# RWKV-7 and top-k experts: quarters of each triangular inverse joined on TensorE, and one fixed order of instructions per engine

## The chip, the cores and the metric

The kernel runs on one core of one Trainium2 chip. The metric is the device time of one execution in microseconds (us), the lower the better. A core has TensorE (PE; its weight loads are listed as PEld), VectorE (DVE), ScalarE (ACT), GpSimd (POOL) and SyncE (SP), which issues most of the DMAs.

## What is computed

Two blocks follow each other. The first is a recurrence over 768 time steps for 4 batches and 8 heads of 40 dimensions:

```python
for t in range(S):
    y[:, :, t] = np.einsum('bhd,bhde->bhe', rt, state)
    Sa = np.einsum('bhde,bhe->bhd', state, at)
    state_decay = state * wt[:, :, None, :] - np.einsum('bhd,bhe->bhde', Sa, bt)
    state = state_decay + np.einsum('bhd,bhe->bhde', vt, kt)
```

Its output, 3072 rows of 320, is the input of the second: each row goes to the expert (of 8) with the largest logit of `x @ w_gate`; each expert keeps the 80 rows with the largest softmax weight; their output is that weight times `relu(x @ w1[e]) @ w2[e]`, and every other row is zero. All is in fp32.

## The kernel before

**Chunks.** The time axis is cut into 12 chunks of T = 64 steps, and two batches (z = 0, 1) lie side by side on the 128 partitions. A unit is one chunk of one pair of batches: 24 units, of which every second one continues the same state. Within a chunk the recurrence becomes linear algebra with a unit triangular system per batch and head. This system is solved by blocks of C = 32: the two 32 x 32 diagonal blocks are inverted, and substitution takes three products (`diagonal(0)`, `below`, `diagonal(1)`).

**Stages of a unit.** `prepare`: transposes of w and a, running products of the decay (`pt`, a scan on VectorE), their reciprocal `ip` (L251), the scaled b and k (`ub`, `kh`, on POOL), their transposes, and the scores against `ahT`, evicted by ACT into `nt` and masked by POOL (L221). `solve`: transposes of r and v, the transposed state (`gT`), the right side (L362, L366), copied to `yy`, the three products (L385, L376, L385), each followed by a copy into `u` (VectorE) or `yy` (ACT), and the new state (L396, L402, L403). `outputs`: the transpose of u, a second set of scores (`lam`, masked on POOL), their products (L441, L448), the multiplication into `xT` (L452), and one matmul (L459) that turns the result back into rows and gives the partial logits. `gate` takes four units at a time: softmax, arg-max, and the largest weights per expert by ten rounds of max and match-replace. It also writes the rows, with the weight as a column, to DRAM.

**Inversion.** Four units together have 128 diagonal blocks (2 batches x 2 blocks x 4 units x 8 heads), one to a partition. `system` writes the blocks from `nt` to DRAM, `invert` reads them back as `lt`, and step i does one product and one sum on VectorE:

```python
nc.vector.tensor_tensor(out=tm, in0=t3[:, 0:i, i : i + 1]..., in1=l3[:, i : i + 1, i + 1 :]..., op=Alu.mult)
nc.vector.tensor_tensor(out=t3[:, 0:i, i + 1 :], in0=t3[:, 0:i, i + 1 :], in1=tm, op=Alu.add)
```

With i = 1 to 30 that is 60 instructions of 30 to 240 elements per partition, six times. The inverse goes to DRAM (`solved`) and comes back as `dt`, laid out for TensorE.

**Order.** The loop over n issues, by `woven`, pieces of `solve(n)`, `outputs(n - 1)`, `prepare(n + 6)`, half an inversion in two of four passes, and a gate. Each list of pieces is spread evenly over the pass. The scheduler of the programming layer sets the final order on each engine, so that blocks of one kind of matmul are often cut by others. In the last passes, `keep_at_work` adds dummy matmuls (L133). Transposes, `gT`, `pp`, the logits and the dummies share two PSUM buffers (`ps_t`).

**End.** After the loop the best weights per expert are merged, slots are computed, rows are gathered by index and the experts' products are done (L715 to L732), with 18 MB of weights loaded in the meantime.

Of the kernel before, what the change touches and what calls it, by code (L numbers as in the profile page):

```python
# [18 lines left out]
def kernel(  # L19
# [26 lines left out]
    nc = tc.nc  # L46
# [24 lines left out]
    XG = 2 * DM - NF * 128  # L71
    XW = XG + 1
# [50 lines left out]
    gates = const.tile([128, NM, E], F32, name="gates")  # L123
    ids = const.tile([128, NM, E], F32, name="ids")
# [11 lines left out]
    with ExitStack() as p1:  # L136
        AHEAD = NG + 2
        NK = AHEAD + 2
        hold = p1.enter_context(tc.tile_pool(name="hold", bufs=1))
        kept = p1.enter_context(tc.tile_pool(name="kept", bufs=NK))  # L140
# [6 lines left out]
        early = dict(w=w, a=a, k=k, b=b)  # L147
        late = dict(r=r, v=v)
# [13 lines left out]
        raw = {n: padded(f"raw_{n}", 2, [128, H, HB], 1.0 if n == "w" else 0.0, dims) for n in (*early, *late)}  # L162
# [4 lines left out]
        state = padded("state", BP, [128, Z, G, 2, HB])  # L167
        og_t = padded("og", 2, [128, NG, 32])
        cand = padded("cand", 2, [128, capr + ZT])

        units = [(c, bp) for c in range(NC) for bp in range(BP)]
        halves = [slice(T * z, T * (z + 1)) for z in range(Z)]

        def load(n, src):
            c, bp = units[n]
            for name, ap in src.items():
                for z in range(Z):
                    nc.sync.dma_start(raw[name][n % 2][halves[z], :, 0:D],
                                      ap[Z * bp + z, :, c * T : (c + 1) * T, :].rearrange("h t d -> t h d"))
# [21 lines left out]

        def scores(lhs, rhs):

            p = ps_s.tile([128, 2, 2, G, T], F32, name="sp", tag="s")
            for i in range(2):
                for g in range(G):
                    for z in halves:
                        for q in range(2):
                            m = slice(HB * q, HB * (q + 1))
                            nc.tensor.matmul(p[z, q, i, g, :], lhsT=lhs[i][m, g, z], rhs=rhs[m, g, z],  # L210
                                             start=True, stop=True)
            return p
# [10 lines left out]

        blocks = nc.dram_tensor("blocks", (NCI, Z, NS, NG, H, C * C), F32, kind="Internal")
        solved = nc.dram_tensor("solved", (NCI, Z, NS, NG, H, C * C), F32, kind="Internal")
        xb_lg = {}
        made = {}
        inverse = {}
        rows_x = {}

        def prepare(n):

            s = {}

            def decays():
                s["raw"] = [raw[x][n % 2] for x in early]
                dec = decay[n % 2]
                nc.scalar.copy(dec[:, :, :, 1:], by_batch(transposed(pairs(s["raw"][0]))))  # L238

                s["pt"] = pt = kept.tile([128, G, Z, T + 1], F32, name="pt", tag="pt")  # L240
                nc.vector.tensor_tensor_scan(flat(pt), flat(dec), flat(begins), 0.0, op0=Alu.mult, op1=Alu.add)  # L241

            def inverted():
                pt = s["pt"]
                p = ps_t.tile([128, G, 2 * D], F32, name="pp", tag="t")
                for g in range(G):
                    for z in range(Z):
                        nc.tensor.matmul(p[halves[z], g, :], lhsT=pt[:, g, z, 1:], rhs=pick[:, 0, 0 : 2 * D],  # L248
                                         start=g == 0, stop=True, skip_group_check=True)
                s["ip"] = ip = sb.tile([128, H, D], F32, name="ip", tag="ip")  # L250
                nc.vector.reciprocal(ip, p.rearrange("p g (q d) -> p (g q) d", q=2))  # L251
                ub, kh = ubs[n % NK], khs[n % NK]
                nc.gpsimd.tensor_tensor(out=ub[:, :, 0:D], in0=s["raw"][3][:, :, 0:D], in1=ip, op=Alu.mult)  # L253
                nc.gpsimd.tensor_tensor(out=kh[:, :, 0:D], in0=s["raw"][2][:, :, 0:D], in1=ip, op=Alu.mult)
                if n + 2 < len(units):
                    load(n + 2, early)

            def decayed_a():
                s["ahT"] = ahT = kept.tile([128, G, ZT], F32, name="ahT", tag="ahT")
                nc.vector.scalar_tensor_tensor(out=by_batch(ahT), in0=by_batch(transposed(pairs(s["raw"][1]))),  # L260
                                               scalar=-1.0, in1=s["pt"][:, :, :, 0:T], op0=Alu.mult, op1=Alu.mult)

            def operand_b():
                s["ubT"] = copied("ubT", pairs(ubs[n % NK]), 1)

            def operand_k():
                s["khT"] = copied("khT", pairs(khs[n % NK]), 1)

            def system():
                nt = kept.tile([128, 2, 2, G, T], F32, name="nt", tag="nt")  # L270
                evicted(nt, scores((s["ubT"], s["khT"]), s["ahT"]))
                masked(nt, slice(1, 2))
                made[n] = s["pt"], s["ahT"], ubs[n % NK], khs[n % NK], nt

                for z in range(Z):
                    for i in range(NS):
                        tt = slice(i * C, (i + 1) * C)
                        p = slice(z * T + i * C, z * T + (i + 1) * C)
                        nc.sync.dma_start(blocks[n // NG, z, i, n % NG].rearrange("h (s t) -> s h t", s=C),
                                          nt[p, 0].rearrange("p q g t -> p (q g) t")[:, :, tt])  # L280
            return [(2, decays), (3, decayed_a), (2, inverted), (2, operand_b), (2, operand_k), (4, system)]

        def invert(k):

            s = {}

            def begin():
                s["lt"] = lt = sb.tile([128, C * C], F32, name="lt", tag="lt", bufs=1)
                nc.sync.dma_start(lt, blocks[k].rearrange("z i u h x -> (z i u h) x"))
                l3 = lt.rearrange("p (s t) -> p s t", s=C)  # L290
                nc.gpsimd.affine_select(out=l3, in_=l3, compare_op=Alu.is_gt, fill=0.0, base=0,
                                        pattern=[[-1, C], [1, C]], channel_multiplier=0)
                s["tt"] = tt = sb.tile([128, C * C], F32, name="tt", tag="tt", bufs=1)
                nc.scalar.copy(tt, lt)  # L294
                nc.gpsimd.memset(tt[:, 0 :: C + 1], 1.0)

            def step(i):
                l3 = s["lt"].rearrange("p (s t) -> p s t", s=C)
                t3 = s["tt"].rearrange("p (s t) -> p s t", s=C)
                n = C - 1 - i  # L300
                tmp = sb.tile([128, C * C // 4], F32, name="tmp", tag="tmp", bufs=1)
                tm = tmp[:, 0 : i * n].rearrange("p (j t) -> p j t", j=i)
                nc.vector.tensor_tensor(  # L303
                    out=tm, in0=t3[:, 0:i, i : i + 1].to_broadcast([128, i, n]),
                    in1=l3[:, i : i + 1, i + 1 :].to_broadcast([128, i, n]), op=Alu.mult)
                nc.vector.tensor_tensor(out=t3[:, 0:i, i + 1 :], in0=t3[:, 0:i, i + 1 :], in1=tm, op=Alu.add)  # L306

            def end():
                nc.sync.dma_start(solved[k].rearrange("z i u h x -> (z i u h) x"), s["tt"])
                inverse[k] = dt_ = sb.tile([128, NG, 2, G, C], F32, name="dt", tag="dt")  # L310
                for z in range(Z):
                    for i in range(NS):
                        p = z * T + i * C
                        nc.sync.dma_start(dt_[p : p + C].rearrange("p u q g t -> p (u q g) t"),
                                          solved[k, z, i].rearrange("u h (s t) -> s (u h) t", s=C))

            return [(3, begin)] + [(1, lambda i=i: step(i)) for i in range(1, C - 1)] + [(1, end)]

        def staggered(first, second, lead):
            first, second = list(first), list(second)
            order = first[:lead]
            for x in range(max(len(first) - lead, len(second))):
                order += first[lead + x : lead + x + 1] + second[x : x + 1]
            return order

        def solve(n):

            c, bp = units[n]
            s = {}
            st = state[bp]

            def reads():
                s["m"] = made[n]
                s["rT"] = copied("rT", pairs(raw["r"][n % 2]))

            def reads_v():
                s["vT"] = copied("vT", pairs(raw["v"][n % 2]))  # L340

# [65 lines left out]
            def loads():  # L407
                if n + 2 < len(units):
                    load(n + 2, late)
# [366 lines left out]
```

## Time and profile before

| | us |
|---|---|
| three runs, lowest / median / highest | 768.96 / 769.78 / 782.09 |
| the profiled execution | 773.57 |
| its span, first to last instruction | 771.9 |
| TensorE busy in it | 601.9 |
| VectorE busy in it | 411.8 |
| mean granted TensorE clock | 0.837 of full |

A row of the timeline has the start, the length, the engine, the line, the operation, what is written and read, the tile of the array (rows x columns), the shape, and how many records are merged; an entry in brackets is idle time before it and what ended it. An fp32 matmul of the smaller tiles appears as two records. The number at the end of a slice is in tenths. Busy time of TensorE overlaps and is no measure of work; the starts of successive blocks are.

### The profile page before, as it was taken

What the parts mean: (1) busy time and instruction counts of PE and PEld (TensorE: products, weight loads), DVE (VectorE), ACT (ScalarE), POOL (GpSimd) and SP (SyncE); (2) the same over time, 40 slices, a digit from 0 to 9 for tenths busy, and PEclk for the clock granted to TensorE, in tenths of its full rate; (3) what the DMA queues carried; (4) which work ended last, traced back from release to release, by engine and by line L of the source; (5) the groups of instructions that cost most, each with busy time, mean ns of one, the idle gap of its engine ahead of it and who ended that gap; (6) DMA issues with size and microseconds to landing.
All of it is one profiled execution on the core that took longest, in us unless ns stands there. A gap on an engine that the chain in (4) does not pass through costs nothing. (4 is left out here: it accounts for less than half of the span.)

```text
span 771.9 us, 28902 instructions
## 1 busy us (share of the span) xinstructions
PE 601.9 (78%) x13042; PEld 504.9 (65%) x13042; DVE 411.8 (53%) x961; ACT 189.5 (25%) x318; POOL 170.2 (22%) x236
## 2 busy tenths in 40 slices
PE   3645528889899767987989796899989941769997
PEld 2534427777788666876878675777868830667775
DVE  5413943598486954787466884558444148200001
ACT  1322122333344222341323332232222210000000
POOL 3331312322223221231233222221111110010111
PEclk9866667899999887996889988788889975657999
DMA  5545553533455145531455333221320018996000
GB/s 86 118 87 101 124 114 51 117 80 76 90 102 89 33 88 100 93 66 26 83 97 97 57 53 76 47 54 20 74 61 12 4 42 260 351 319 197 24 18 16
DMA packets 224911, 69.50 MB, mean 90 GB/s; under 512 B 205332, under 2 KB 219796, under 8 KB 224788
## 3 DMA queue, kind: packets, MB, share of 16 engines
q1 hardware_dynamic: 216640, 57.18, 35.0%
q10 hardware_dynamic: 7380, 8.68, 3.8%
q8 instruction: 102, 1.67, 0.9%
q0 software_dynamic: 768, 1.81, 0.8%
q14 instruction: 21, 0.17, 0.1%
HBM read 51.85 MB, written 15.77 MB: 88 GB/s over the span
## 5 line engine op out<-in xcount | busy, mean ns | idle before, releaser
L221 POOL TENSOR_SCALAR_AFFINE_SELECT lam<-lam 64x1024 f32<-64x1024 f32 x48 | 55.5, 1155 | 238.7 <-ACT lam L215 237.1
L303 DVE TENSOR_TENSOR tmp<-tt,lt 128x30 f32<-128x30 f32 (+9 forms) x180 | 72.7, 404 | 14.0 <-ACT tt L294 9.3
L306 DVE TENSOR_TENSOR tt<-tt,tmp 128x30 f32<-128x30 f32 (+9 forms) x180 | 74.5, 414 | 5.6 <-DVE tmp L303 0.5
L385 PE MATMUL pr<-yy,dt 32*32 32x40 f32 x1536 | 45.8, 211 | 21.6 <-DMA dt<-solved 10.2
L251 DVE RECIPROCAL ip<-pp 128x320 f32<-128x320 f32 x24 | 51.6, 2150 | 16.4 <-PE pp L248 16.4
L221 POOL TENSOR_SCALAR_AFFINE_SELECT nt<-nt 64x512 f32<-64x512 f32 x48 | 32.9, 685 | 111.4 <-ACT nt L215 106.0
L385 PEld LDWEIGHTS pr<-yy,dt 32*32 32x32 f32 x1536 | 37.3, 117 | 30.4 <-ACT yy L378 12.0
L194 PE MATMUL tp<-ident,ub 128*128 128x128 f32 x96 | 20.7, 353 | 44.4 <-POOL ub L253 44.4
L387 DVE COPY u<-pr 128x320 f32<-128x320 f32 x48 | 23.4, 488 | 55.7 <-PE pr L385 53.4
L734 DVE TENSOR_SCALAR y<-yp,rows 80x320 f32<-80x320 f32 x8 | 4.4, 547 | 77.7 <-PE yp L732 77.7
L452 DVE TENSOR_TENSOR xT<-yp,pt 128x512 f32<-128x512 f32 x24 | 16.5, 687 | 53.5 <-PE yp L448 53.5
L194 PEld LDWEIGHTS tp<-ident,ub 128*128 128x128 f32 x96 | 13.2, 174 | 47.8 <-POOL ub L253 47.7
L241 DVE TENSOR_TENSOR_SCAN pt<-decay,begins 128x520 f32<-128x520 f32 x24 | 30.3, 1261 | 23.5 <-ACT decay L238 23.3
L448 PE MATMUL yp<-lam,kh 64*64 64x64 f32 x768 | 35.8, 248 | 7.7 <-POOL lam L221 7.5
L732 PE MATMUL yp<-w,hT 128*80 128x320 f32 x128 | 38.8, 452 | 0.0
L448 PEld LDWEIGHTS yp<-lam,kh 64*64 64x64 f32 x768 | 27.5, 150 | 15.0 <-POOL lam L221 10.3
L715 PEld LDWEIGHTS hp<-xe,w 128*128 128x128 f32 x256 | 36.1, 227 | 1.4 <-DVE xe L707 1.3
L726 ACT ACTIVATE hT<-hp 128x320 f32<-128x320 f32 x16 | 6.1, 435 | 125.7 <-DMA w<-in_moe_w_dram 63.8
L715 PE MATMUL hp<-xe,w 128*128 128x80 f32 x256 | 36.3, 311 | 0.0
L199 ACT COPY ubT<-tp 128x512 f32<-128x512 f32 x24 | 14.0, 585 | 87.0 <-PE tp L194 87.0
L215 ACT COPY nt<-sp 128x1024 f32<-128x1024 f32 x24 | 24.3, 1012 | 39.2 <-PE sp L210 31.2
L210 PE MATMUL sp<-rT,vT 64*64 64x64 f32 x768 | 31.5, 233 | 3.0 <-ACT nt L215 3.0
(344 smaller groups left out, 1288.6 us busy)
## 6 DMA issues: line engine op xcount, KB each, us to landing
w<-in_moe_w_dram SPq DMA_DIRECT2D x8, 1280.0 KB, 14.7
w<-in_moe_w_dram SPq DMA_DIRECT2D x8, 1024.0 KB, 16.2
x_rows<-xb ACTq DMA_DIRECT2D x48, 96.2 KB, 2.5
raw_w<-in_w_dram SPq DMA_DIRECT2D x48, 80.0 KB, 2.9
raw_a<-in_a_dram SPq DMA_DIRECT2D x48, 80.0 KB, 3.4
raw_k<-in_k_dram SPq DMA_DIRECT2D x48, 80.0 KB, 2.8
raw_b<-in_b_dram SPq DMA_DIRECT2D x48, 80.0 KB, 2.8
out_dram<-zero ACTq DMA_DIRECT2D x8, 480.0 KB, 4.1
```

The source lines that it names most:

```text
L194: nc.tensor.transpose(p[:, g, :], t[:, g, :], ident)
L210: nc.tensor.matmul(p[z, q, i, g, :], lhsT=lhs[i][m, g, z], rhs=rhs[m, g, z], start=True, stop=True)
L215: nc.scalar.copy(o.rearrange("p i q g t -> p q i (g t)"), p.rearrange("p q i g t -> p q i (g t)"))
L221: nc.gpsimd.affine_select(out=oo, in_=oo, compare_op=Alu.is_gt, fill=0.0, base=0, pattern=[[0, oo.shape[1]], [1, T]], channel_multiplier=-1)
L241: nc.vector.tensor_tensor_scan(flat(pt), flat(dec), flat(begins), 0.0, op0=Alu.mult, op1=Alu.add)
L251: nc.vector.reciprocal(ip, p.rearrange("p g (q d) -> p (g q) d", q=2))
L303: nc.vector.tensor_tensor(out=tm, in0=t3[:, 0:i, i : i + 1].to_broadcast([128, i, n]), in1=l3[:, i : i + 1, i + 1 :].to_broadcast([128, i, ...
L306: nc.vector.tensor_tensor(out=t3[:, 0:i, i + 1 :], in0=t3[:, 0:i, i + 1 :], in1=tm, op=Alu.add)
L385: nc.tensor.matmul(pr[m, h, :], lhsT=dt_[m, n % NG, h % 2, h // 2, :], rhs=s["yy"][m, h, :], start=h == 0, stop=True, skip_group_check=True)
L448: nc.tensor.matmul(s["y"][HB * q : HB * (q + 1), z, g, :], lhsT=x[halves[z], 2 * g + q, :], rhs=s["lam"][halves[z], o, q, g, :], start=Fal ...
L715: nc.tensor.matmul(hp[f // (FK // 2)][:, f % (FK // 2), :], lhsT=t1[:, i, f * 128 : (f + 1) * 128], rhs=xe[:, i, :], start=f % (FK // 2) = ...
L732: nc.tensor.matmul(yp, lhsT=hT[:, f, :], rhs=w2[:, f, :], start=f == 0, stop=f == FK - 1)
```

## The change

- **Quarters.** Each 32 x 32 block's two 16 x 16 diagonal quarters are inverted, side by side in one instruction: `step` runs for i = 1 to 14. If A and D are the inverted quarters and B the corner between them, the missing corner is the product A B D. Two sets of 32 small matmuls for each unit form it: `joint_n` (with `an`, the transpose of A, which goes through DRAM as `solved_n`) and `joint`, whose result is added into `dt`.
- **Order.** `do(f, ...)` gives each instruction of TensorE, VectorE, ACT and POOL a dependence on the one before it on its engine. The loop is a list of `do` calls, in which parts of one tiling shape stand together. SP's order is still the scheduler's.
- **State.** The state has 64 columns per pair of heads and not 128; the new state is one addition on VectorE and one product on POOL. A second copy, `state_b`, in the form that the right side needs, is made by two ACT copies (`spread`).
- **Rest.** Units are prepared five passes ahead and not six. Rows are written to DRAM in each pass, by SP, without the weight; the weight comes with the token number out of one matmul of twice the columns. The first loads are issued by SP and ACT in turn. The dummy matmuls in the loop are gone; those after it stay.

The core of the diff:

```diff
+        Q = C // 2
+        state = padded("state", BP, [128, Z, G, HB], 0.0, lambda t: t)
+        state_b = padded("state_b", BP, [128, Z, G, 2, D])
-            return [(3, begin)] + [(1, lambda i=i: step(i)) for i in range(1, C - 1)] + [(1, end)]
+        def step(k, i):
+            l4, t4 = quarters(inverse[k]["lt"]), quarters(inv_t)
+            n = Q - 1 - i
+            nc.vector.tensor_tensor(
+                out=tm, in0=t4[:, :, 0:i, i : i + 1].to_broadcast([128, 2, i, n]),
+                in1=l4[:, :, i : i + 1, i + 1 :].to_broadcast([128, 2, i, n]), op=Alu.mult)
+            nc.vector.tensor_tensor(out=t4[:, :, 0:i, i + 1 :], in0=t4[:, :, 0:i, i + 1 :], in1=tm, op=Alu.add)
+        def end(k):
+            nc.sync.dma_start(solved[k]..., inv_t[:, 0 : C * C])
+            nc.scalar.copy(inv_n[:, :, 0:Q], quarters(inv_t)[:, 0].rearrange("p s t -> p t s"))
+            nc.sync.dma_start(solved_n[k]..., inv_n...)
+            # for each of the four blocks: an <- solved_n, dt <- solved
+        def joint_n(n):
+            for h, z, i in tiles32:
+                m = block(z, i)
+                mq = slice(m.start, m.start + Q)
+                nc.tensor.matmul(p[m, h, :], lhsT=nt[mq, 0, h % 2, h // 2, i * C : (i + 1) * C],
+                                 rhs=an[mq, n % NG, h % 2, h // 2, :], ...)
+            nc.scalar.copy(na, p)
+        def joint(n):
+            for h, z, i in tiles32:
+                nc.tensor.matmul(p[m, h, :], lhsT=na[m, h, :], rhs=dt_[m, n % NG, h % 2, h // 2, Q:], ...)
+            nc.vector.tensor_tensor(out=o, in0=p..., in1=o, op=Alu.add)
+        def do(f, *args):
+            ...
+                        tc.add_manual_dep(i, latest[i.engine], ..., reason="order")
-            lists += [prepare(m) for m in coming if m < NU]
-            woven(*lists)
+        for n in range(NU + 1):
+            o, m = n - 1, n + AHEAD
+            # in this order, each if it is due:
+            operands(m), spread(o)
+            # n % 4 == 1: a gate; 3: steps 5 to 14 and end; else: rounds of max
+            rows(o), system(m), reads_g(n), right(n), inverted(m + 1), turned(o)
+            diagonal(n, 0), lower(o), reads(n, r), reads(n, v), below(n)
+            joint_n(n + 1), decays(m + 2), decayed_a(m + 1), diagonal(n, 1), joint(n + 1)
+            # n % 4 == 2: begin of the next inversion
+            summed(o), to_state(n), products(m + 2)
+            # n % 4 == 2: steps 1 to 4
+            logits(o), fill(n - 2)
-                nc.tensor.matmul(ip, lhsT=hot[:, m - m0, :], rhs=ids[:, m, :], ...)
+                nc.tensor.matmul(ip, lhsT=hot[:, m - m0, :], rhs=ig[:, m].rearrange("p i e -> p (i e)"), ...)
-        nc.vector.tensor_scalar_mul(y, yp, rows[e][:, XG : XG + 1])
+        nc.vector.tensor_scalar_mul(y, yp, weight[:, e : e + 1])
```

## The prediction

> **What bounds the kernel now.** I read the page first (shares, slices, costliest groups), then the busy table by stage, then TensorE's timeline of one clean slot, then the timeline around the first use of an inverse. A slot is one pass of the loop over n; its marker is the logits matmul (L459), which for unit k stands in slot k+1.
>
> ```profile
> span 771.9 us, 28902 instructions
> PE 601.9 (78%) x13042; PEld 504.9 (65%) x13042; DVE 411.8 (53%) x961; ACT 189.5 (25%) x318; POOL 170.2 (22%) x236
> PEclk9866667899999887996889988788889975657999
> L303 DVE TENSOR_TENSOR tmp<-tt,lt 128x30 f32<-128x30 f32 (+9 forms) x180 | 72.7, 404 | 14.0 <-ACT tt L294 9.3
> L306 DVE TENSOR_TENSOR tt<-tt,tmp 128x30 f32<-128x30 f32 (+9 forms) x180 | 74.5, 414 | 5.6 <-DVE tmp L303 0.5
> ```
>
> The inversion (L303, L306) is 147 of VectorE's 412 us. The stage table, cut at the first diagonal product, at unit 0's, 15's and 23's logits:
>
> ```profile
> core 0: us, PE busy (x) PEld busy (x) DVE busy (x) ACT busy (x) POOL busy (x), PEclk, DMA share, GB/s
> 0.00:112.70 112.70, 52.52 (x837) 42.39 (x837) 58.52 (x111) 25.26 (x38) 32.77 (x72) 0.76 0.52 104
> 112.70:135.60 22.90, 19.12 (x528) 16.64 (x528) 7.46 (x11) 4.54 (x8) 3.96 (x4) 0.75 0.38 63
> 135.60:473.50 337.90, 289.46 (x7654) 250.32 (x7647) 239.21 (x526) 113.56 (x186) 90.22 (x109) 0.88 0.42 80
> 473.50:625.50 152.00, 137.24 (x3388) 114.08 (x3380) 70.29 (x201) 39.36 (x68) 26.86 (x30) 0.89 0.18 37
> 625.50:771.90 146.40, 103.59 (x651) 81.46 (x651) 36.30 (x112) 6.78 (x18) 16.38 (x21) 0.75 0.52 162
> ```
>
> The prelude (112.7 us) leaves TensorE idle for more than half; the fifteen full slots take 22.5 us each with TensorE busy for 19.3; the last eight take 19.0. So the loop is TensorE's, with 2 to 4 us of waits and cold clock per slot. Inside a clean slot, 306.91 to 325.71 (18.8 us, about 1.0 of it waiting), the blocks read:
>
> ```profile
> 316.90 0.68 PE L396 MATMUL pr<-raw_v,kh 64*64 64x40 f32 x32
> 317.39 0.53 PE L396 MATMUL pr<-u,ub 64*64 64x40 f32 x21
> ...
> 320.45 0.66 PE L194 MATMUL tp<-ident,raw_w 128*128 128x128 f32 x4
> 320.94 0.60 PE L194 MATMUL tp<-ident,raw_v 128*128 128x128 f32 x4
> 321.47 0.33 PE L210 MATMUL sp<-rT,vT 64*64 64x64 f32 x4
> 321.78 0.66 PE L194 MATMUL tp<-ident,u 128*128 128x128 f32 x4
> ```
>
> From start to start, 32 records on four 64*64 tiles take 0.49 us (15 ns each), four transposes 0.49. But four score records between transposes hold TensorE for 0.31, against 4 x 19 ns for their like in a long run: one visit to another tiling shape costs about 0.23 us, 0.12 per switch. The slot has 21 switches. And the first inverse:
>
> ```profile
> 107.25 0.21 DVE L306 TENSOR_TENSOR tt<-tt,tmp 128x30 f32<-128x30 f32 x1
> 107.49 0.35 SPq L309 DMA_DIRECT2D solved<-tt  x1
> 110.38 2.18 SPq L314 DMA_DIRECT2D dt<-solved  x4
> 112.67 0.34 PE L385 MATMUL pr<-yy,dt 32*32 32x40 f32 x2 [8.89 <-DMA dt<-solved]
> ```
>
> The steps ran from 71.4 to 107.5, spread among other units' VectorE work, and TensorE waited for their result.
>
> [...] the trace has 1.0 in clean slots and 0.80 in 287 to 316 us, where TensorE idles 4.6 us.
>
> **The change, part by part.**
>
> *Inversion.* 60 VectorE instructions per group become 28. Each handles at most 112 elements, and the like in the uncontended stretch (104.7 to 107.5) stand 0.24 to 0.32 us apart: about 8.0 us per group instead of 147/6 = 24.5. Off VectorE: 6 x 16.5 = 99 us. None of this counts by itself; it counts where VectorE was late.
>
> *Joining the quarters.* Each slot gains 64 matmuls, 128 records, on 32-row tiles. Nearest rows: 15 ns a record on four tiles (L396), 22 on two (L385, 32 records in 0.70). That is 1.9 to 2.8 us; I take 2.2. Evictions: an ACT copy (0.4) and a VectorE add (about 0.5), both beside TensorE.
>
> *Order by shape.* Counting runs of one shape in the new slot gives 11 switches instead of 21: -1.2 us. Interleaving by shape no longer fills waits, so waits must be walked through. Normal slot, from the end of the previous logits: the second transpose needs the PSUM buffer that the ACT copy (0.43) and VectorE reduction (0.19) must read: late by 0.6. Then rows, scores, state reads, right side; the copy of yy (0.43) is hidden by pp and the u transpose; the reciprocal (2.15) ends at about 9.8 us, when the r transpose, wanting its buffer, comes at 10.1; the u copy follows at 10.3, wanted at 11.1; the lam masks (2 x 1.155 on POOL after ub and kh) end near 13.9, wanted at 16. All covered, some by 0.3 us. Sum: 17.8 of work - 1.2 + 2.2 + 0.6 = 19.4 us.
>
> *Slot 4k+1 (gate).* The transpose of og now stands in front of the rows. Its chain takes 2.4 us in the tail of before (reduction at 627.5 to og at 629.9); TensorE waits 2: 21.4.
>
> *Slot 4k+3 (end of an inversion).* The scan and steps 1 to 4 precede the logits reduction (3.4 us), steps 5 to 14 follow (6.1 us), so the steps end at about 9.7. ACT's order puts the copy into inv_n ahead of the nt eviction, gT and yy: the u transpose comes at about 12 instead of 7.6, 4.3 late. Then solved and solved_n go out (2.8 us), eight reads are issued at 0.55 each behind two blocks DMAs, an lands at about 18, and joint_n is wanted at 16: 2 more. With about 1.3 for the colder clock: 27.0.
>
> A group of four slots is 19.4 + 21.4 + 19.4 + 27.0 = 87.2, 21.8 each. Slots 2 to 16 are three such groups and 19.4, 27.0, 19.4: 327 against 338, **-11**. Slots 17 to 24 lose the preparation (4.0 us of TensorE work) by degrees: 20.9, 17.8, 24.5, 15.3, 17.3, 15.3, 13, 10 = 134 against 152, **-18**. The dummy matmuls of these slots (140 records, 26.6 us, partly filling waits) go; the remaining work keeps TensorE dense.
>
> *Prelude.* pp now precedes the next w transpose, and the first loads leave from two queues. At the cold clock a unit is a chain of about 8.7 us (transposes 1.1 each, decay copy 0.6, scan 1.24, pp 1.3, scores 2.2); unit 3's nt comes at about 43 (48.7 before), and SP is not stuck until 58 with its blocks. But POOL's order has unit 4's masks ahead of the begin: begin ends near 61.5, 28 steps to 69.7, the DRAM trip with its ten DMAs to 79, joints to 83, slot 0 up to the first diagonal (6 warm, 10 cold) to 91 against 112.7. From there to unit 0's logits: 7.5 + 19.4 = 26.9 against 22.9. Net **-18**, bounds -8 and -26.
>
> *State, x_rows, gate weight.* Compact state makes acc and its product one instruction each (was two of 0.49 each); two ACT copies per slot appear, hidden; the product on POOL (0.87 by L253) precedes the next state read by 4 us. x_rows writes move to SP, two per slot of 0.65; SP's list for a slot is about 11 us, in order of need. The final gate chain saves POOL's og copy and pays a weight copy: **-0.5**, bounds -2 and +2.
>
> Sum: -11 - 18 - 18 - 0.5 = -48. The profiled execution took 773.57 (span 771.9): 726. The median of the runs is 769.78, 3.8 lower; I carry the difference over: **722 us**.
>
> **Rivals.** (1) Slots 4k+3 stay dense, because the late evictions are absorbed: 6 x 7.6 us less, 676. For it: VectorE would be under 14 us in every slot. Against it: ACT's order is strict, and the copy into inv_n needs the last step. (2) Little but the prelude gains: joints at the upper 2.8, and a cold clock in the last six slots without their dummy matmuls, 3.7 each (a quarter of 15); 0.6 x 22 + 22 = 35: 757, no measurable change. For it: those matmuls fill waits there now; against: the work between the waits is dense. (3) Slower: the cover inside the fixed order fails in every slot. The place is the chain diagonal, u, below, yy, diagonal, u. Bare, it can be read at 563.2 to 568.4, where TensorE waits 0.58, 1.67 and 0.66 = 2.9 us; with 0.6 for the reciprocal in front and clock loss it is 3.5 per slot, 23 x 3.5 = 80: 802. It decides from 2.1 us per slot beyond my walk (48/23). For it: slacks of 0.3 to 0.8 us; against: three of five blocks that cover it are over 1 us long, and a late step delays its followers equally.
>
> **How the numbers follow.** Forecast 0.62, its own range 698 to 750; rival 1 0.12, rival 2 0.11, rival 3 0.15. The range 685 to 765 leaves out rival 3 and part of rival 1. A measurement of this kernel tells about 2% from no change. Faster: 0.62 + 0.12; same: 0.11; slower: 0.15, with the rounding 0.74, 0.11, 0.15.
>
> **What would show it.** Right: logits spaced 19 to 20 us in slots 4k+2 and 4k, 26 to 28 in 4k+3, with TensorE idle for ACT's gT or yy and for DMA an; steps near 0.29 us; na and dn about 1.1 us each; the first diagonal at 85 to 97. Wrong: spacing over 23 in ordinary slots, or idle time before below and diagonal in each of them; na over 2 us; a first diagonal after 105.

## The result and the profile after

The changed kernel takes 810.47 us (median of four runs, 807.08 to 814.68) beside 769.37 for the kernel before on the same chip: a ratio of 1.054, 95% interval 1.048 to 1.061. It is 5% slower; 722 was predicted, with a range up to 765. The profiled execution took 807.08. From its page (span; TensorE's row and VectorE's; the granted clock by slices):

```profile
span 805.3 us, 34678 instructions
PE 601.7 (75%) x15974; PEld 526.9 (65%) x15974; DVE 292.4 (36%) x730; ACT 208.4 (26%) x386; POOL 197.4 (25%) x278
PEclk9965787859899797976989768886778865566999
```

VectorE is relieved as meant, 411.8 to 292.4 us. TensorE has 2932 records more and is busy as long as before, in a longer span. The costliest inversion rows and the busy table, cut as before at the first diagonal product and at unit 0's, 15's and 23's logits:

```profile
L313 DVE TENSOR_TENSOR tmp<-inv_t,lt 128x28 f32<-128x28 f32 (+6 forms) x84 | 22.5, 268 | 9.9 <-POOL inv_t L303 7.4
L316 DVE TENSOR_TENSOR inv_t<-inv_t,tmp 128x28 f32<-128x28 f32 (+6 forms) x84 | 20.9, 249 | 2.9
```

```profile
core 0: us, PE busy (x) PEld busy (x) DVE busy (x) ACT busy (x) POOL busy (x), PEclk, DMA share, GB/s
0.00:93.00 93.00, 44.35 (x806) 35.95 (x808) 39.95 (x79) 20.30 (x31) 28.63 (x65) 0.74 0.65 97
93.00:123.40 30.40, 25.48 (x940) 22.72 (x940) 10.28 (x13) 10.32 (x19) 8.49 (x9) 0.89 0.42 69
123.40:501.70 378.30, 300.71 (x9665) 270.53 (x9664) 155.77 (x370) 125.84 (x232) 113.14 (x143) 0.83 0.47 86
501.70:659.20 157.50, 128.21 (x3922) 116.31 (x3919) 49.73 (x155) 45.16 (x86) 31.17 (x41) 0.77 0.22 40
659.20:805.30 146.10, 102.93 (x649) 81.42 (x649) 36.63 (x113) 6.78 (x18) 15.96 (x20) 0.75 0.50 158
```

Up to unit 0's logits the change gains 12 us (135.6 to 123.4). Slots 2 to 16 lose 40 (337.9 to 378.3), slots 17 to 24 lose 6 (152.0 to 157.5), the end is unchanged. In slots 2 to 16 the mean granted clock fell from 0.88 to 0.83. In this trace the logits' matmul takes 275 ns (median of 8) at 299.7, where the clock is 1.00, and 421 ns at 348.8, where it is 0.50. The waits of TensorE (total, times, longest):

```profile
PE na L342 <- DMA an<-solved_n: 46.8, 24, 17.8
PE pr L416 <- issue: 22.3, 14, 2.4
PE gp L520 <- DVE og L513: 20.4, 6, 4.4
...
PE yp L459 <- issue: 11.3, 6, 2.9
...
PE dn L353 <- issue: 9.8, 10, 2.0
...
PE pr L404 <- ACT yy L389: 2.6, 1, 2.6
```

Three things stand out. na waits for `an`: 21.0 of the 46.8 us before the loop, 17.8 of them at once, and 25.9 in the loop. The gate's transpose waits for og six times. And "issue", where nothing that the profile shows was missing: 44.7 us over all rows of this view, against 1.4 in the kernel before. A clean slot shows what that is:

```profile
293.78 0.36 PE L353 MATMUL dn<-dt,na 32*32 32x16 f32 x20
294.97 0.53 PE L353 MATMUL dn<-dt,na 32*32 32x16 f32 x40 [0.83 <-issue]
295.43 0.69 PE L459 MATMUL yp<-lam,kh 64*64 64x64 f32 x32
295.94 0.65 PE L459 MATMUL yp<-lam,ub 64*64 64x64 f32 x32
296.41 0.51 PE L416 MATMUL pr<-raw_v,kh 64*64 64x40 f32 x24
298.97 0.33 PE L416 MATMUL pr<-raw_v,kh 64*64 64x40 f32 x8 [2.05 <-issue]
```

TensorE stops in the middle of a block, its operands long there. Between the two stops stand 40 + 32 + 32 + 24 = 128 records, 256 instructions (a record is a weight load and a matmul). The page's table of DMA queues (packets, MB, share) has a queue q8 of kind "instruction", first before, then after:

```profile
q8 instruction: 102, 1.67, 0.9%
```

```profile
q8 instruction: 125, 2.05, 1.1%
```

Each packet is 16 KiB. 2 x 13042 records are 101.9 times 256 instructions, 2 x 15974 are 124.8 (and so in every experiment, as in e4 with 134 packets for 133.9): by these counts the queue brings TensorE's program, 16384 / 256 = 64 bytes an instruction. The page does not show when packets start, but the trace holds it. Around the clean slot they start at 288.69, 292.24, 296.38 and 300.28 us, nowhere in the trace closer than 3.34 us. All 29 stops of over 0.3 us that this trace puts to "issue" end 2.2 to 2.9 us after the start of such a packet, while in slots 2 to 16 the packets start 5.0 us apart on average. **Theory A, supply:** TensorE gets a block of 256 instructions in 3.34 us at best, the closest spacing of these packets; a slot had 4.03 blocks and now has 5.03, and the 128 records of the joints are so short (na's 64 take 0.7 us) that they are used up faster than they come. **Theory B, the trip for `an`** and the waits behind it. **Theory C, the gate in front.** **Theory D:** the fixed order itself is worse than the woven one.

In what follows, "ordinary" slots are 4k+2 and 4k, means over slots 2 to 16: 22.1 and 21.3 in the changed kernel.

### The profile page after: what moved, and what is told of

The parts are those of the page before. It is cut to its first block, busy times and chain, and to the rows that moved or that the text cites. A ratio compares the mean times of both kernels' runs of the same rounds, so it can differ in the third digit from the quotient of the medians.

```text
span 805.3 us, 34678 instructions
## 1 busy us (share of the span) xinstructions
PE 601.7 (75%) x15974; PEld 526.9 (65%) x15974; DVE 292.4 (36%) x730; ACT 208.4 (26%) x386; POOL 197.4 (25%) x278
## 5 line engine op out<-in xcount | busy, mean ns | idle before, releaser
L421 POOL TENSOR_TENSOR state<-acc,pt 128x320 f32<-128x320 f32 x22 | 30.0, 1363 | 164.4 <-DVE acc L420 142.2
L342 PE MATMUL na<-an,nt 16*32 16x32 f32 x1536 | 25.3, 205 | 47.1 <-DMA an<-solved_n 46.8
L342 PEld LDWEIGHTS na<-an,nt 16*32 16x32 f32 x1536 | 20.2, 115 | 50.8 <-issue 25.1
L260 DVE SCALAR_TENSOR_TENSOR ahT<-tp,pt 128x512 f32<-128x512 f32 x24 | 16.6, 691 | 92.6 <-PE tp L205 92.0
L404 PE MATMUL pr<-yy,dt 32*32 32x40 f32 x1536 | 40.3, 206 | 4.5 <-ACT yy L389 2.6
L406 DVE COPY u<-pr 128x320 f32<-128x320 f32 x48 | 22.5, 469 | 52.0 <-PE pr L404 51.1
L450 PE MATMUL yp<-rT,gT 64*64 64x64 f32 x768 | 41.2, 286 | 0.0
L274 POOL TENSOR_TENSOR ub<-raw_b,ip 128x320 f32<-128x320 f32 x24 | 21.6, 898 | 80.0 <-issue 38.2
L450 PEld LDWEIGHTS yp<-rT,gT 64*64 64x64 f32 x768 | 37.1, 194 | 5.7 <-issue 5.5
L256 DVE TENSOR_TENSOR_SCAN pt<-decay,begins 128x520 f32<-128x520 f32 x24 | 29.6, 1232 | 22.8 <-ACT decay L250 22.7
L804 PEld LDWEIGHTS hp<-xe,w 128*128 128x128 f32 x256 | 36.1, 227 | 1.4 <-DVE xe L796 1.3
L823 DVE TENSOR_SCALAR y<-yp,weight 80x320 f32<-80x320 f32 x8 | 4.4, 547 | 77.5 <-PE yp L821 77.5
L227 ACT COPY lam<-sp 128x1024 f32<-128x1024 f32 x24 | 24.3, 1013 | 30.6 <-PE sp L222 30.6
```

The source lines that it names most:

```text
L227: nc.scalar.copy(o.rearrange("p i q g t -> p q i (g t)"), p.rearrange("p q i g t -> p q i (g t)"))
L256: nc.vector.tensor_tensor_scan(flat(pt), flat(decay[n % 2]), flat(begins), 0.0, op0=Alu.mult, op1=Alu.add)
L274: nc.gpsimd.tensor_tensor(out=ub[:, :, 0:D], in0=raw["b"][n % 2][:, :, 0:D], in1=ip, op=Alu.mult)
L342: nc.tensor.matmul(p[m, h, :], lhsT=nt[mq, 0, h % 2, h // 2, i * C : (i + 1) * C], rhs=an[mq, n % NG, h % 2, h // 2, :], start=h == 0, sto ...
L404: nc.tensor.matmul(o["pr"][m, h, :], lhsT=dt_[m, n % NG, h % 2, h // 2, :], rhs=o["yy"][m, h, :], start=h == 0, stop=True, skip_group_chec ...
L406: nc.vector.tensor_copy(us[n % 2][:, :, 0:D], o["pr"])
```

## The experiments

The diffs are shortened. The kernel before was measured anew beside each experiment, with medians from 765 to 774 us, so a difference between kernels that were not measured together is uncertain by up to these 9 us.

**e1: no joints.**

```diff
-            if n + 1 < NU:
-                do(joint_n, n + 1)
...
-            if n + 1 < NU:
-                do(joint, n + 1)
```

> The changed kernel without both joint products (na and dn with their evictions); the off-diagonal quarter of each inverse stays zero, so this part of the computation is left out. Each slot issues 516 TensorE records again instead of 644, 4.03 blocks of 256 instructions instead of 5.03. Fetch theory (TensorE's instructions arrive at no more than one block in 3.3 to 4.1 us, and the fixed order puts its short records together): the waits that the profile puts to issue, 44 us, fall below 15; the work of the joints, 23 x 1.4 = 32, and the waits of na for an, 47, go as well, though the reads of the other quarters arrive no earlier, so that 15 of them come back at the diagonal product: 690 to 720 us. Inverse-trip theory (the lost time is the wait for an and little else): the issue waits stay at 30 or more, and the time is 735 to 760. The rest of the change being the loss (order by shape, gate in front): over 770.

Measured: 696.11 us (0.909 of before, 0.900 to 0.918). Ordinary slots 17.5 and 17.1, issue waits 12.9. The missing corner is left out, so this kernel shows a price and is no replacement. The rest of the change is a gain of about 70 us, and the joints cost about 114. D is not settled by this alone, since the short inversion is part of the gain; e8 and e9 below keep the fixed order with the whole inverse on VectorE and are no slower than before (0.982 and 0.938), so D falls.

**e2: joints with half the records.**

```diff
-    lhsT=nt[...], rhs=an[...]   # and lhsT=na[...], rhs=dt_[...]
+    lhsT=high(nt[...]), rhs=high(an[...])   # upper halves, as bf16
```

> The changed kernel with the operands of both joint products read as the upper half of each 32-bit word (bf16), so that the same 64 products take 64 records a slot instead of 128; the products are coarser for it. All waits for an, all evictions and the order stay. Fetch theory: half a block of 256 instructions less in each slot, at 4.05 us a block 2.0 us a slot, 23 slots: -45 us, and issue waits below 30. Work theory (records cost what they hold TensorE for, 11 ns each in na): 64 x 11 ns = 0.7 us a slot, -16 us. Inverse-trip theory: the slots 4k+3 are bound by an, so the gain is only in the other three of four: -12.

Measured: 746.56 us, 64 less than the changed kernel, where supply said 45 and work 16. Ordinary slots 19.2 and 19.1, issue waits 20.0. The 4.05 us a block was the author's estimate; around the clean slot above the packets stand 3.55 to 4.14 us apart. The waits for `an` stayed (48.0), so B can't be what this took away. The products are coarser, and fewer records are less work too; e12 separates the two.

**e3: the whole gate behind below.**

```diff
-                do(prob); do(weig); do(candi)      # ahead of rows
+                # the three behind below(n)
```

> The changed kernel with the gate of the slots 4k+1 (its transpose on TensorE and the VectorE and ACT work before it) behind the below products instead of in front of the rows. Gate theory: TensorE's waits for og, 20.4 us, fall below 4, and the time by 15 to 20 us. Fetch theory: the wait in front lets the next blocks of instructions come in, so the time lost there is partly lost again at the next block edge: -3 to -10 us, with issue waits up from 44.

Measured: 794.36 us, 16 less, but not as expected: the waits for og stayed at 18.1, since the VectorE and ACT work was moved together with the transpose. This edit therefore does not test C; e10 does. The issue waits fell to 27.8, and the ordinary slots too (20.8 and 20.5). Why moving a gate does that is open.

**e4: the rate of supply by itself.**

```diff
+        def stretch(times, cols):
+            for _ in range(times):          # four tiles of 64 x 64 in turn
+                ... nc.tensor.matmul(burst[...], lhsT=src[..., 0:64], rhs=src[..., 0:cols], start=True, stop=True)
+        stretch(256, 40); stretch(128, 80); stretch(128, 160)
```

> The kernel before with three stretches of independent fp32 matmuls ahead of its work, on four tiles of 64 x 64, whose results nobody reads: 1024 matmuls of 40 columns (2048 records, 16 blocks of 256 instructions), 512 of 80 columns (1024 records, 8 blocks), 512 of 160 columns (8 blocks). Fetch theory: the first stretch takes 53 to 65 us, that is 26 to 32 ns a record where short runs show 15, with gaps at multiples of 128 records; the second 27 to 33 us; the third is bound by its columns, at 40 to 50 ns a record. Engine-rate theory: the first stretch goes on at 15 ns a record (31 us), the second at about 22 (23 us), without gaps.

Measured (899.83 us for the whole, one run): 27.5, 27.2 and 33.9 ns a record. The 22 ns for 80 columns and the 40 to 50 for 160 were the author's estimates. The timeline of the second stretch:

```profile
65.33 2.44 PE L146 MATMUL burst<-src 64*64 64x80 f32 x128 [0.39 <-issue]
69.06 2.44 PE L146 MATMUL burst<-src 64*64 64x80 f32 x128 [1.29 <-issue]
72.51 2.44 PE L146 MATMUL burst<-src 64*64 64x80 f32 x128 [1.01 <-issue]
75.97 2.44 PE L146 MATMUL burst<-src 64*64 64x80 f32 x128 [1.01 <-issue]
```

128 records in 2.44 us, a stop, the next 128: a period of 3.45 us, which is also the spacing of the instruction packets there (3.39 to 3.75). Forty and eighty columns cost the same; 160 take longer (4.35 us per 128), without a stop in the timeline, and the packets follow at about that distance (4.17 to 4.56). So the supply measured here is 256 instructions in 3.45 us, 27 ns a record. The first stretch has the same rate in another form: an even 107 ns per four records, and only four places where 0.3 to 0.7 us pass from one start to the next, multiples of 128 records apart. The expectation had a stop at every block there; why it is even is not settled.

**e6: the joints' number of records in the order of before.**

```diff
+        def extra():                      # 32 matmuls of 32 x 32 x 32 on constants
+            ...
+            if n + 1 < NU:
+                lists.append([(1, extra), (1, extra)])
```

> The kernel before, with 64 more fp32 matmuls of 32 x 32 x 32 (128 records, the number of the joints) in each of slots 0 to 22, woven into its order in two groups of 64 records; nobody reads their result. Fetch theory: a slot then needs 5.03 blocks of instructions, at 3.45 us a block 17.4 us, and where short records stand together the blocks come late: +2.6 us a slot (what half the joints cost in the fixed order, taken once, because the woven order has slow transposes between) to +4.7 (what the joints cost there), so +60 to +108 us, with waits put to issue of over 15 us, where before has 1.4. Work theory: 128 records at 11 ns, 1.4 us a slot, +32 us, and no issue waits.

Measured: 804.75 beside 765.12 us (1.054, 1.047 to 1.061): +38 to 40, 1.7 a slot, near the work (32) and under the 60 to 108 that supply forecast; only the issue waits came (16.3). In the profile, slots 2 to 16 grow by 21.0 us, and the added matmuls hold TensorE for 21.3 (the time from the end of the work before a block to its own end). This profile is of the fastest of the four executions, at a clock of 0.854 beside 0.837 in that of before, so 21.0 is probably on the low side. Part of the price is hidden: TensorE's waits for ub fall from 44.4 us to 26.7, so the added records stand in part where it had waited anyway. At 22.5 us a full slot, 5.6 a block, the kernel before leaves supply some room.

**e7: the joints at the head of the next slot.**

```diff
+            if now: do(joint_n, n)        # ahead of rows(o)
+            if now: do(joint, n)          # ahead of reads_g(n)
```

> The changed kernel with both joint products of unit n moved from the end of slot n-1 into slot n: na ahead of the rows, dn ahead of the state reads. Same instructions, other order. Inverse-trip theory: an is wanted some 10 us later, so the waits for it in the loop (29 us) go, the quarter is ready for the diagonal product at mid-slot: -25 to -30 us. Fetch theory: the loop needs the same blocks; na and dn no longer stand among below, the lam products and the state products, so that fewer short records follow each other there, but they now meet rows and reads: the waits for an turn partly into issue waits, -10 to -25 us. If both hold, the slots 4k+3 fall from 31 to about 26 and the others stay at 21 to 23.

Measured: 775.19 us, 35 less. Slots 4k+3 fall from 31.5 to 25.4, ordinary ones stay (21.6 and 22.2), waits for `an` are 8.0 in all. B is real, and it lies in the slots 4k+3: 24 of the 27 us by which slots 2 to 16 shrink. Not all of the 6.1 us a slot is the trip: in e13 below, the same shift of matmuls that wait for no `an` shortens these slots by 2.3.

**e8: the whole inverse on VectorE, in the fixed order.**

```diff
-                for i in range(5, Q - 1): do(step, new, i)     # two 16 x 16 quarters
+                steps_of(9, 16)     # 32 x 32; 16 to 30 at three later places of slot 4k+3
-                do(joint_n, n + 1) ... do(joint, n + 1)
```

> The changed kernel with the whole inverse back on VectorE (30 steps of up to 240 elements instead of 14 of up to 112), no joints, no solved_n and an; order by shape, compact state and the gate stay. The steps stand spread over the slots 4k+2 and 4k+3. It computes everything. Beside the kernel without the joints (696 us) it pays 16.5 us of VectorE work more per group: in the prelude all of it (first diagonal +13), in the loop only what is late. Fetch theory: as few instructions as the kernel before, so the order by shape is no loss: 705 to 735, faster than before. Order theory (the fixed order itself costs time, by late operands): 750 to 790.

Measured: 750.0 us (0.982, 0.976 to 0.989), above the 735 that supply allowed and at the lower edge of what late operands in the fixed order were given: TensorE waits 36.1 us for u behind the steps, and the slots 4k+3 take 32.8. The ordinary ones take 17.9 and 18.1.

**e9: the same, prepared earlier.**

```diff
-        AHEAD = NG + 1
+        AHEAD = NG + 2              # begin and steps 1 to 6 in slot 4k+1, 7 to 15 in 4k+2, the rest in 4k+3
-                do(candi)           # ahead of rows
+                do(candi)           # behind below(n)
```

> As the run with the whole inverse on VectorE in the fixed order, with each unit prepared six slots ahead instead of five, so that the 30 steps of a group spread over the end of slot 4k+1 and the slots 4k+2 and 4k+3; in the prelude units 5 and 6 are prepared between the steps of the first inverse; the transpose of og stands behind below, while its VectorE and ACT work stays in front. It computes everything. Order theory as it now stands (the fixed order is dense when its operands are in time, and needs 4.03 blocks of instructions a slot): the waits for u (36 us), for ub in the prelude (25) and for og (21) fall to a few us each: 680 to 705, all full slots at 17 to 20 us. If VectorE's steps then delay reciprocal, ahT or u in another place: 720 to 745.

Measured: 723.52 us (0.938, 0.932 to 0.944). That is the second of the two ranges: VectorE's steps are late in another place. Slots 4k+2 take 25.9, 4k and 4k+1 18.5 and 17.9. It computes everything in the precision of before and is faster than both kernels.

**e10: e7 with the gate's transpose behind below. e11: that with bf16 joints.**

```diff
-                do(weig); do(candi)
+                do(weig)            # candi behind below(n)
```

> As the run with both joint products moved into the next slot, with only the transpose of og (and its copy into the candidates) behind below; its VectorE and ACT work stays in front, so that og is ready when TensorE comes to it. Gate theory: the 20.9 us of waits for og go, the slots 4k+1 fall from 24.6 to about 22: 752 to 760. If the time returns as issue waits or as a later wait of the same slot: 768 to 778.

> As the run with the joints in the next slot and the late transpose of og, with the operands of the joints read as bf16 (64 records a slot instead of 128, coarser products). Fetch theory with grouping: in this order the records that go are worth less than the 2.8 us a slot of the changed kernel's own order, because issue waits are 18 us and not 44: 10 to 35 us less than the run beside it. Pure work: 16 us less. If the price of a record is the same in every order: 64 less.

Measured: 760.32 us (0.987, 0.981 to 0.993) and 719.98 (0.933, 0.926 to 0.939). The waits for og are gone but for one of 3.0 us, and the slots 4k+1 fall from 24.6 (e7) to 21.8: C is real and worth 15 us by the medians, 20 by the shares of before (1.014 and 0.987). The 64 records are worth 40 us, more than the 10 to 35 expected and less than 64.

**e12 and e13: the joints' instructions without their data.**

```diff
-                do(joint_n, n + 1) ... do(joint, n + 1)
+                do(extra) ... do(extra)     # the matmuls of e6; e12: in the same places, e13: at the head
```

> The changed kernel without its joints (the off-diagonal quarter of each inverse is left out), and in the two places where they stood two groups of 64 records of 32 x 32 x 32 fp32 matmuls on constants, in slots 0 to 22, whose results nobody reads: the joints' instructions without their operands, evictions and the trip for an. Fetch theory: the price in the ordinary slots stays what the joints cost, 17.3 to 20.5 or 21.5 us, with issue waits of 30 us or more: 696 + 23 x 3.2 to 4.2 = 770 to 793. Dependency theory (the joints are dear through what they wait for and who waits for their evictions): 17.3 + 1.4 to 1.8 us, 728 to 738, and issue waits as without the joints.

> The same as the run with unused matmuls in the joints' places, with the two groups at the head of the slot, ahead of the rows and ahead of the state reads. Fetch theory with grouping (the price depends on how many short records stand together): the lam and state products no longer follow them, but rows and reads do, so less than in the joints' places: 745 to 770. Fetch theory without grouping (the price is the number of blocks alone): as in the joints' places within 8 us. Dependency theory: 728 to 738 as well.

Measured: e12 772.13 us, 76 more than e1, e13 752.98. In e12 the ordinary slots are back at 21.8 and 21.2. Its longest lists of issue waits:

```profile
PE pr L424 <- issue: 21.1, 14, 3.2
...
PE na L364 <- issue: 18.1, 15, 2.5
PE yp L467 <- issue: 17.9, 9, 3.5
```

Issue waits are 60.0 us in all. The added matmuls read constants and nobody reads them; they need no more than a free PSUM buffer. In the eight ordinary slots of 2 to 16 issue waits are 2.9 us a slot, beside 0.6 in e1, and the 36 stops of over 0.3 us end 2.2 to 3.6 us after the start of an instruction packet. This decides for A in the ordinary slots. e13 is in the range that grouping gave, but its ordinary slots (21.2 and 21.5) are those of e12; its gain is in the slots 4k+3 (23.6), 5 us up to unit 0's logits and 4 in the last eight slots. Grouping isn't shown to matter, nor excluded: the issue waits fall to 39.1 us, but the added matmuls now wait 7.9 us for ACT's copies of ubT and khT, which may be what keeps the ordinary slots as long. The sum of the issue waits is thus a sign of the cause and not its price.

## Where the time went

As shares of the kernel before measured beside them, e1 is 0.909, e12 1.005 and the changed kernel 1.054. Of 769 us that is -70 from before to e1, +74 from e1 to e12 and +38 from e12 to the changed kernel. The first is the fixed order, the short inversion and the prelude; the second the supply of 128 more records a slot, with their work; the third what the real joints add, mostly the trip for `an`: the slots 4k+3 are 25.9 in e12 and 31.5 in the changed kernel.

Of e12's loss against e1 in slots 2 to 16 (46.2 us), the added matmuls hold TensorE for 21.6, idle time grows by 11.5, and the other blocks of matmuls take 13 more, most of it in logits (16.4 to 20.5), state products (16.0 to 20.3) and rows (19.6 to 22.8), which stand behind the stops. The clock in these slots is 0.92 in e1, 0.88 in e12. That the stops cost more than their own length, by a lower clock, is the author's estimate from these figures; no run kept the clock up to show it.

An ordinary slot takes 4.3 us per block of instructions in nearly all fixed orders: e1 17.3 / 4.03, e11 19.3 / 4.53, e12 21.5 / 5.03, changed 21.7 / 5.03. This is a description, not a rate of the hardware: it lies above the 3.45 of e4.

## Why the prediction was wrong

- *The step that failed: "Joining the quarters".* It priced 128 records at 15 to 22 ns each from rows of 32 records, 2.2 us, bound 2.8. Their hold on TensorE was overpriced if anything (1.7 in slots 2 to 16); the cost in ordinary slots is 4.4 (21.7 against 17.3 in e1). The sum had no term for the supply of instructions: one block more a slot is 3.45 us at the rate of e4. The price was read from runs of 32 records, a quarter of a block; 27 ns is the rate that lasts over many blocks (e4). The queue q8 was on the page of before and its packets in the trace, 3.43 us apart at the closest, while 128 of the forecast's own 15 ns records last 1.9 us. The forecast did not use them.
- *The order by shape came out.* Without the joints the walk gives 17.8 - 1.2 + 0.6 = 17.2 us; e1 shows 17.3. The changed kernel has the 11 switches that were counted. That each saves 0.12 us is the author's estimate from the four score records between transposes (0.31 us against 4 x 19 ns) and is in this sum alone; no run changes the switches by themselves.
- *Ordinary slots* were put at 19.4 and took 21.7. Over fifteen slots that 2.3 is 34 us of the 51 by which slots 2 to 16 missed. 21.7 lies between the forecast's sign of being right (19 to 20) and that of being wrong (over 23), and waits put to "issue" were not among its signs.
- *Slots 4k+3:* put 7.6 over an ordinary slot, measured 9.8, with the parts wrong. The 1.3 us for a colder clock was the author's estimate: in before the mean granted clock is 1.00 in 306.91 to 325.71 and 0.80 in 287 to 316 us; in the changed kernel it is 0.71 in the slots 4k+3 up to 15 and 0.91 in the ordinary ones, and what that costs no run shows by itself. In slot 11 the steps end at +9.9 (forecast 9.7) and the transpose of u comes at +12.1 (about 12), but TensorE idles there for 1.3 us and not 4.3, since it comes late itself. The last `an` lands at +23.7 and not +18: the reads are issued from +14.6 on and take 3.4 to 4.6 us each, and na, half issued, waits for one after the other, 6.8 us in all where 2 were put:

```profile
358.74 0.35 SPq L319 DMA_DIRECT2D solved<-inv_t  x1
...
367.57 0.22 PE L342 MATMUL na<-an,nt 16*32 16x32 f32 x2 [2.56 <-DMA an<-solved_n]
...
372.55 1.06 PE L342 MATMUL na<-an,nt 16*32 16x32 f32 x58 [1.70 <-DMA an<-solved_n]
```

- *Slots 4k+1:* put 2.0 over an ordinary slot, measured 4.5. The waits for og are 3.4 us each and not 2. That is 1.4 of the 2.5 us; the rest is open.
- *Slots 17 to 24:* 134 forecast, 157.5 measured; e1 has 131.2 and e12 151.1, so most of it comes with the 128 records, by their work and their supply, at a clock of 0.77 (before: 0.89).
- *Prelude and end:* first diagonal 93.0 (forecast 91), -12 of the -18 up to unit 0's logits, end -0.3. VectorE's steps of 0.25 to 0.27 us were right.
- *Rival 3* came near in size (802) and is wrong in mechanism: below and the diagonals wait 3.4 us in all for their operands, not in every slot. *Rival 1* failed, but only in part on what was held against it: in the slots 4k+3 up to 15 TensorE waits 4.4 to 6.8 us for `an` and 0.3 to 1.3 for gT behind the copy into inv_n; *rival 2* had the joints at 2.8 a slot, still too cheap; that the last slots run at a colder clock without their dummy matmuls was an estimate, and e1, which has none there either, shows 8 to 9 tenths in the whole slices of slots 17 to 24.

Waits put to "issue" come to 1.4 us in the kernel before and to 60.0 in e12; in the second stretch of e4 TensorE stops for 1.0 us after each 2.44 us of records.

## What to carry to other kernels

Count the instructions that TensorE gets per stage and hold them against the supply: here 256 in 3.45 us, 27 ns per pair of weight load and matmul (e4). Where many short matmuls stand together, they are priced at that rate and not at that of a short run (here 15 ns). Fewer records (bf16 operands, 64 records a slot where fp32 has 128) were then worth more than their own time (40 us in e11 beside e10, where their work was put at 16), and a shorter chain on VectorE bought with many small products lost (292.4 us of VectorE work instead of 411.8, 810 us in all instead of 769). Waits put to "issue" in the middle of a run of one kind of matmul, about a whole number of 128 records apart (128 in the clean slot and in e4), were the sign.

## What was not expected of the hardware

- A matmul of 80 columns costs no more than one of 40 in a long run (27.2 and 27.5 ns a record, e4).
- 128 records more a slot cost 1.7 us in the kernel before (e6) and about 3.3 in the fixed order (e12). In the former they stand in part where TensorE had waited for ub.
- Reading the joints' operands as bf16 (e11 beside e10) took 40 us, 5%, from a kernel in which those products hold TensorE for 1.6 us a slot.
